# A fused delta-rule attention and MLP kernel: first keys loaded alone, weights and later chunks held back behind the first transposes, first chunk prepared in halves, PSUM banks of its own for the MLP

## The chip, the cores and the metric

The kernel runs on one core of one Trainium2 chip. The metric is the device time of one execution in microseconds (us). Each time in this text is the median of several executions; a profile is one execution of the same program and gives its span, the time from the first to the last recorded instruction, which is about 2 us shorter than the time. The engines are TensorE (PE in the profile, with its weight loads as PEld), VectorE (DVE), ScalarE (ACT), GpSimd (POOL) and SyncE (SP), whose only work here is to issue DMAs.

## The reference, cut to what matters

```python
# 4 x 8 heads, 768 steps, head size 48; x is 3072 x 384
k_n = k / (norm(k, axis=-1) + 1e-06)
for t in range(768):                       # per head
    y[t]  = q[t] @ state
    state = state + beta[t] * outer(k_n[t], v[t] - state.T @ k_n[t])
x = y as rows of tokens, 8 heads side by side        # 3072 x 384
h = x @ w_in                                         # 384 x 2048
out = gelu_tanh(h) @ w_out                           # 2048 x 384
```

The kernel computes the recurrence in 12 chunks of 64 steps. Within a chunk it inverts a small triangular matrix per head with 64x64 matmuls (two groups of heads, five rounds each). Every two chunks give 512 tokens, which the MLP can take as one tile, so there are 6 MLP tiles. The inputs are float32; the matmuls take bfloat16, and the 4-byte weights are cast on their way into SBUF.

## The kernel before

The program builds a list of operations, each with an estimated cost for each engine that may run it, what it reads and writes, and a priority. A list scheduler, at build time, then fixes **one order for each engine**. On the chip every engine goes through its order and waits, in order, on semaphores. So an instruction whose data is late holds up everything behind it on its engine. This holds for SP too: a DMA that must wait for its source, or for its buffer to be free, holds up all later DMAs of that queue.

```python
def load_step(c, pr):                       # keys, queries, values of chunk c; 3 buffers (RL = 3)
    s = c % RL
    for nm, t, src in (("kf", kf, k), ("qf", qf, q), ("vf", vf, v)):
        ...
        for a in range(2):                  # 2 DMAs of 192 KB each
            op({"sp": 0.6}, {"sp": f_dma(t[s][64 * a:64 * a + 64, :, :], sv[a, C * c:C * c + C, :, :])},
               writes=[f"{nm}{s}_{a}"], prio=pr, dma=f"d_{nm}{c}", lat=4.0)
...
load_step(0, -70)
... # beta
load_step(1, -60)
for kt in range(KT):                        # 3 DMAs issued by POOL, cast to bf16
    op({"pool": 1.2}, {"pool": f_dma(W1[:, kt, :], w1v[:, kt, :])}, writes=[f"W1{kt}"],
       prio=T(0, 15 + kt), dma="d_w1", lat=8.0)
for j in range(2):                          # 2 more
    op({"pool": 1.2}, {"pool": f_dma(W2[:, 8 * j:8 * j + 8, :], w2v[:, 8 * j:8 * j + 8, :])},
       writes=[f"W2{j}"], prio=T(0, 20 + j), dma="d_w2", lat=8.0)
...
def prep(c):        # square keys, reduce, root, reciprocal; KQ = normalised keys and queries in bf16
    ...
    op({"sp": 1.1}, {"sp": f_dma(KQT[i]..., KQ[i]..., True)},      # DMA transpose, 3 buffers (RB = 3)
       reads=[f"KQ{i}", f"KQq{i}"], writes=[f"KQT{i}"], prio=pr + 0.2, dma=f"d_T{c}", lat=4.0)
...
def mlp(t):
    pr = T(2 * t + 2, 0)                    # due when chunk 2t + 2 is
    ... # DMA transpose x -> xT, then 16 groups of 3 matmuls xT,W -> gelu -> gT, then gT,W2 -> out
...
prep(0)
prep(1)
for c in range(NCH):
    if c + 2 < NCH:
        load_step(c + 2, T(c - 1))          # nothing but its buffer and the order holds it back
        prep(c + 2)
    masks(c)
    for g in range(2):
        intra(c, g)                         # the 64x64 matmuls
    state(c)
    if c % 2 == 1:
        mlp(c // 2)
```

Below, T0, T1, T2 and T3 are the DMA transposes of the first four chunks' keys and queries (KQT<-KQ in the profile). No attention matmul of a chunk can start before its transpose has landed.

## Time and profile before

The time before was 345.34 us, the median of 3 runs (343.79 to 346.5).

The span cut in three, from the view of busy time by stretches. The cuts are the first attention matmul (the first that reads KQT) and the first MLP matmul (the first xT,W). A row gives the stretch in us, its length, then busy time and number of instructions of each engine, the granted TensorE clock as a share of full speed, the busy share of the 16 DMA engines, and GB/s. The DMA share is a sum of packet times and exceeds 1 in places here.

```profile
core 0: us, PE busy (x) PEld busy (x) DVE busy (x) ACT busy (x) POOL busy (x), PEclk, DMA share, GB/s
0.00:41.30 41.30, 1.69 (x10) 1.40 (x14) 6.87 (x21) 8.05 (x11) 13.71 (x19) 1.00 1.11 180
41.30:102.30 61.00, 38.47 (x1632) 34.85 (x1632) 41.68 (x65) 27.50 (x47) 34.49 (x23) 0.91 0.64 108
102.30:340.90 238.60, 226.67 (x5476) 137.16 (x5472) 132.48 (x201) 133.91 (x229) 72.22 (x49) 0.98 0.39 75
```

Three stages show. In the **head** (41.3 us) TensorE has only the small transposes of beta and the DMA engines are full. In the **ramp** (61.0 us) there is only attention work, and TensorE is busy 38.5 us of it. In the **rest** (238.6 us) MLP matmuls fill the gaps of the attention and TensorE is busy 226.7 us, 95%. Only there is it the bound.

What happens in the head, from the timeline of the kernel before (start, length in us, engine, line, instruction, output<-input; in brackets the idle time before it and what ended it; lines of SPq and POOL with DMA_ are DMAs being issued, not moved):

```profile
0.81 1.44 SPq L304 DMA_DIRECT2D kf<-in_k_dram  x2
1.78 1.86 POOL L304 DMA_DIRECT2D W<-in_moe_w_in_dram  x3
2.29 9.43 SPq L304 DMA_DIRECT2D qf<-in_q_dram  x2
3.61 1.82 POOL L304 DMA_DIRECT2D W<-in_moe_w_out_dram  x2
11.77 9.14 SPq L304 DMA_DIRECT2D vf<-in_v_dram  x2
15.20 0.84 ACT L289 ACTIVATE sq<-kf 128x768 f32<-128x768 f32 x1 [13.11 <-DMA kf<-in_k_dram]
36.22 3.45 SPq L303 DMA_TRANSPOSE KQT<-KQ  x1
41.26 1.07 PE L296 MATMUL ps<-KQT 48*64 48x128 bf16 x32 [12.20 <-DMA KQT<-KQ]
45.85 3.65 SPq L303 DMA_TRANSPOSE KQT<-KQ  x1
51.98 3.66 SPq L303 DMA_TRANSPOSE KQT<-KQ  x1
```

The first keys are issued at 0.81 us and can be used only at 15.20 us. The two issues of queries take 9.43 us of the SP queue, those of values 9.14 us. The weights are on their way at that time.

The end of the kernel, from the chain of waits (the work that ended last, followed back; start, length, what): the last MLP tile waits for its transpose with nothing else to do.

```profile
311.59 0.80 ACT x L289
312.41 0.81 ACT x L289
313.24 3.70 DMA xT<-x
316.99 20.95 PE ps L296 x112
```

### The profile page before, as it was taken

How to read it: one execution, taken by the hardware profiler on the slowest of the kernel's cores; microseconds unless marked ns; L12 is line 12 of the kernel's file. 1: busy time of each engine (PE TensorE's matmuls, PEld its weight loads, DVE VectorE, ACT ScalarE, POOL GpSimd, SP SyncE). 2: the span in 40 equal slices, each digit the busy share in tenths (PEclk: the TensorE clock that was granted, in tenths of full speed). 3: DMA queues.
4: the chain of work that ended last, by engine and by line, in shares of the span. 5: the costliest groups of instructions: out<-in, count | busy, mean ns of one | idle time of the engine just before them, and what ended most of it. 6: DMA issues, size and time to landing. Idle time of an engine off the chain costs nothing.

```text
span 340.9 us, 15121 instructions
## 1 busy us (share of the span) xinstructions
PE 266.8 (78%) x7110; PEld 173.4 (51%) x7110; DVE 181.0 (53%) x287; ACT 169.5 (50%) x286; POOL 120.4 (35%) x90
## 2 busy tenths in 40 slices
PE   0001125875769999898999699999999999999896
PEld 0001015764754556554567455566666655656353
DVE  2102255786774757676676554666757756642001
ACT  1202312665459753477534386554795447852640
POOL 5007266443679616057432660160252105000000
PEclk9999999999678999999999699999999999999999
DMA  7999999200899723937414923228042060002201
GB/s 132 193 195 190 189 193 185 44 6 11 139 165 178 133 49 94 177 73 115 91 50 65 193 45 64 50 64 184 10 53 38 26 96 4 4 4 69 71 23 70
DMA packets 116078, 31.83 MB, mean 93 GB/s; under 512 B 110512, under 2 KB 115632, under 8 KB 116016
## 3 DMA queue, kind: packets, MB, share of 16 engines
q1 hardware_dynamic: 113504, 27.73, 45.8%
q0 software_dynamic: 2512, 3.15, 5.3%
q8 instruction: 55, 0.90, 1.1%
q14 instruction: 7, 0.06, 0.1%
HBM read 20.64 MB, written 4.72 MB: 74 GB/s over the span
## 4 chain that ended last, share of the span: by engine, by line
PE 66%; SPq 12%; DMA 8%; ACT 5%; issue 3%; DVE 3%; POOL 1%
PE ps L296 64%; SPq L304 9%; DMA kf<-in_k_dram 7%; SPq L303 2%; ACT Z L289 2%; PE ps L571 2%; ACT x L289 1%; ACT sq L289 1%; DVE F L280 1%; DMA xT<-x 1%; POOL W L280 1%; DVE N L280 1%; DVE R L280 1%; POOL sq L280 0%; POOL Z L280 0%
## 5 line engine op out<-in xcount | busy, mean ns | idle before, releaser
L280 DVE TENSOR_TENSOR F<-twoI,ps 128x512 bf16<-128x512 bf16 x120 | 80.1, 683 | 55.1 <-PE ps L296 54.5
L296 PE MATMUL ps<-xT,W 128*128 128x512 bf16 x288 | 76.5, 391 | 1.7 <-DMA xT<-x 1.4
L289 ACT ACTIVATE Z<-ps 128x512 bf16<-128x512 f32 x96 | 55.3, 597 | 39.1 <-PE ps L296 38.7
L296 PE MATMUL ps<-W,gT 128*128 128x384 bf16 x384 | 69.2, 327 | 0.0
L289 ACT ACTIVATE gT<-ps 128x512 bf16<-128x512 f32 x96 | 56.8, 598 | 22.5 <-PE ps L296 21.0
L296 PE MATMUL ps<-X,Z 64*64 64x64 bf16 x1920 | 52.8, 201 | 8.9 <-ACT Z L289 4.8
L296 PE MATMUL ps<-Z,F 64*64 64x64 bf16 x1920 | 54.1, 201 | 7.2 <-issue 5.0
L280 POOL TENSOR_TENSOR W<-identB,N 128x512 bf16<-128x512 bf16 x21 | 24.2, 1151 | 95.3 <-DVE N L280 95.3
L296 PEld LDWEIGHTS ps<-Z,F 64*64 64x64 bf16 x1920 | 42.6, 115 | 28.7 <-DVE F L280 16.4
L296 PEld LDWEIGHTS ps<-X,Z 64*64 64x64 bf16 x1920 | 42.5, 116 | 25.0 <-ACT Z L289 13.9
L296 PEld LDWEIGHTS ps<-W,gT 128*128 128x128 bf16 x384 | 34.4, 98 | 22.0
L280 POOL TENSOR_TENSOR sr<-ss,half 128x16 f32<-128x16 f32 x9 | 26.4, 2932 | 29.1 <-DVE ss L478 29.1
L296 PEld LDWEIGHTS ps<-xT,W 128*128 128x128 bf16 x288 | 22.9, 99 | 24.5 <-issue 1.9
L285 DVE COPY osb<-ps 128x384 f32<-128x384 f32 x23 | 12.8, 557 | 39.0 <-PE ps L296 38.8
L289 ACT ACTIVATE sq<-kf 128x768 f32<-128x768 f32 x9 | 7.6, 842 | 42.9 <-DMA kf<-in_k_dram 42.9
L289 ACT ACTIVATE x<-ps 64x768 bf16<-64x768 f32 x24 | 19.3, 804 | 15.7 <-PE ps L296 15.3
L296 PE MATMUL ps<-KQT 48*64 48x128 bf16 x384 | 12.5, 246 | 18.5 <-DMA KQT<-KQ 17.5
L280 POOL TENSOR_TENSOR NU<-mU,bcol 128x1024 f32<-128x1024 f32 x12 | 23.7, 1976 | 1.0 <-DVE bcol L285 1.0
L289 ACT ACTIVATE TT<-ps 128x512 bf16<-128x512 f32 x24 | 14.1, 595 | 18.7 <-PE ps L296 18.6
L296 PE MATMUL ps<-identF,BL 128*128 128x128 f32 x6 | 1.6, 448 | 27.4 <-DMA BL<-in_beta_dram 27.4
L280 POOL TENSOR_TENSOR KQ<-kf,rn 128x768 bf16<-128x768 f32 x12 | 17.7, 1474 | 15.1 <-PE ps L296 9.8
L280 DVE TENSOR_TENSOR N<-ps,NU 128x512 bf16<-128x512 f32 x24 | 16.3, 686 | 11.8 <-PE ps L296 11.7
(48 smaller groups left out, 224.1 us busy)
## 6 DMA issues: line engine op xcount, KB each, us to landing
kf<-in_k_dram SPq DMA_DIRECT2D x24, 192.0 KB, 4.2
qf<-in_q_dram SPq DMA_DIRECT2D x24, 192.0 KB, 4.6
vf<-in_v_dram SPq DMA_DIRECT2D x24, 192.0 KB, 4.5
out_dram<-osb SPq DMA_DIRECT2D x24, 192.0 KB, 2.8
W<-in_moe_w_in_dram POOLq DMA_DIRECT2D x3, 512.0 KB, 8.6
W<-in_moe_w_out_dram POOLq DMA_DIRECT2D x2, 768.0 KB, 17.8
BL<-in_beta_dram SPq DMA_DIRECT2D x2, 96.0 KB, 4.5
KQT<-KQ SPq DMA_TRANSPOSE x12, 5.3
```

The source lines that it names most:

```text
L280: return lambda e: e.tensor_tensor(out() if callable(out) else out, a() if callable(a) else a, b() if callable(b) else b, op)
L285: return lambda e: e.tensor_copy(out, a() if callable(a) else a)
L289: return lambda e: e.activation(out, a() if callable(a) else a, func)
L296: ins = t.matmul(out, lhsT, rhs, start=st, stop=sp_, skip_group_check=skip)
L303: return lambda e: e.dma_start_transpose(out, a)
L304: return lambda e: e.dma_start(out, a)
L571: ins = t.transpose(bankb()[r, p, :], W[r, p, :], identB[r, :])
```

## The change

The intent was to start the attention early. The first keys are loaded alone, then beta, queries and the next keys. Weights wait: W1 for the second transpose (T1), W2 for the third (T2). The other loads of chunks 0 to 2 wait for the preparation of chunk 0 or 1. The first chunk is squared and multiplied in two halves on two engines. The MLP goes to the lowest priority and gets two PSUM banks of its own (6 for attention), all 8 for the last tile. The scheduler also gets a simple model of DMA bandwidth. The diff, cut to its core:

```diff
+BANKS = {"t": (0, 6), "f": (6, 8), "l": (0, 8)}
 ...
+            if o.dma:                                   # in the scheduler: transfers one after the other
+                dma_free = max(o.end + 1.3, dma_free) + o.bw
+                o.lat = dma_free + 0.5 - o.end
 ...
-        load_step(0, -70)
+        load("kf", 0, -70)
 ...     # beta
-        load_step(1, -60)
-        ... # W1 and W2 with no wait
+        load("qf", 0, -68)
+        load("kf", 1, -67)
 ...
+            parts = [slice(0, 8), slice(8, 16)] if c == 0 else [slice(0, NP)]
+            ... # square on ACT and POOL, product on DVE and POOL, one half each, for chunk 0
 ...
-            op(dict(d_pool2(512), dve=0.4), {"pool": ... W ...})        # and the same for Z
+            op({"dve": 0.42} if c < 2 else d_pool2(512), {"pool": ... W ...})
 ...
-            pr = T(2 * t + 2, 0)
+            pr = T(2 * t + 2, 1000)
+            mo = "f" if t < NT - 1 else "l"
 ...
         prep(0)
+        load("qf", 1, -40, ["KQ0", "KQx0", "KQq0"])                     # wait for chunk 0's keys and queries
+        load("vf", 0, -39, ["KQ0", "KQx0", "KQq0"])
         prep(1)
+        load("kf", 2, -38, ["KQ0", "KQx0", "KQq0"])
+        load("qf", 2, -37, ["KQ0", "KQx0", "KQq0"])
+        for kt in range(KT):
+            op({"pool": 0.9}, {"pool": f_dma(W1[:, kt, :], w1v[:, kt, :])}, reads=["KQT1"], writes=[f"W1{kt}"],
+               prio=-20 + kt, dma="d_w1", bw=2.8)
+        load("vf", 1, -15, ["KQ1", "KQq1"])
         for c in range(NCH):
             if c + 2 < NCH:
-                load_step(c + 2, T(c - 1))
+                for nm in ("kf", "qf", "vf"):
+                    if c > 0 or nm == "vf":
+                        load(nm, c + 2, T(c - 1), ["KQ1", "KQq1"] if c == 0 else [])
                 prep(c + 2)
+            if c == 0:
+                for j in range(2):
+                    op({"pool": 0.9}, {"pool": f_dma(W2[...], w2v[...])}, reads=["KQT2"], writes=[f"W2{j}"],
+                       prio=-5 + j, dma="d_w2", bw=4.2)
```

More of the change, by code (lines that the diff above doesn't have):

```diff
@@ L21 @@
     __slots__ = ("idx", "cost", "fns", "deps", "prio", "alloc", "uses", "dma", "lat",
-                 "eng", "start", "end", "count", "clock", "sync", "mode")
+                 "eng", "start", "end", "count", "clock", "sync", "mode", "bw")
 class Plan:
@@ L38, in __init__, with op @@
         self.users = {}
-    def op(self, cost, fns, reads=(), writes=(), prio=0.0, alloc=(), dma=None, lat=0.0, mode="t"):
+    def op(self, cost, fns, reads=(), writes=(), prio=0.0, alloc=(), dma=None, lat=0.0, mode="t", bw=0.0):
         o = Op()
         o.idx = len(self.ops)
-        o.cost, o.fns, o.prio, o.dma, o.lat, o.mode = cost, fns, prio, dma, lat, mode
+        o.cost, o.fns, o.prio, o.dma, o.lat, o.mode, o.bw = cost, fns, prio, dma, lat, mode, bw
         o.alloc = tuple(alloc)
@@ L89, in schedule @@
         pe_mode = "t"
+        dma_free = 0.0
         bank_free = [0.0] * self.nbanks
@@ L100, in dep_time, with find_banks @@
             return t
-        def find_banks(n, t0):
+        def find_banks(n, t0, lo, hi):
             best = None
-            for i in range(self.nbanks - n + 1):
+            for i in range(lo, hi - n + 1):
                 ts = bank_free[i:i + n]
@@ L135, in schedule @@
                                 bank_free[k] = None
-                            f = find_banks(n, t)
+                            f = find_banks(n, t, *BANKS[o.mode])
                             for k, x in sv:
@@ L148, in schedule @@
                     pr = o.prio
-                    if e == "pe" and o.mode != pe_mode:
+                    if e == "pe" and (o.mode == "t") != (pe_mode == "t"):
                         pr += KEEP
@@ L162, in schedule @@
             o = ops[i]
-            if e == "pe" and o.mode != pe_mode:
+            if e == "pe" and (o.mode == "t") != (pe_mode == "t"):
                 t += SWITCH
@@ L413, in bass_deltanet__then__act_gelu_tanh_kernel @@
             op({"dve": 0.7}, {"dve": lambda e, i=i: e.memset(KQ[i][:, :, :, D:64], 0.0)},
-               writes=[f"KQ{i}"], prio=-90 + i)
+               writes=[f"KQz{i}"], prio=-90 + i)
         const("identF", identF, 0.0, ALU.not_equal, 1.0, [[-1, 128]], 1)
@@ L425, in bass_deltanet__then__act_gelu_tanh_kernel, with load @@
            reads=IDI, writes=["twoI"], prio=-80)
-        def load_step(c, pr):
+        def load(nm, c, pr, after=()):
+            t, src = {"kf": (kf, k), "qf": (qf, q), "vf": (vf, v)}[nm]
             s = c % RL
-            for nm, t, src in (("kf", kf, k), ("qf", qf, q), ("vf", vf, v)):
-                sv = src.rearrange("b h s d -> (b h) s d").rearrange("(p a) s d -> a s p d", a=2)
-                for a in range(2):
-                    op({"sp": 0.6}, {"sp": f_dma(t[s][64 * a:64 * a + 64, :, :], sv[a, C * c:C * c + C, :, :])},
-                       writes=[f"{nm}{s}_{a}"], prio=pr, dma=f"d_{nm}{c}", lat=4.0)
+            sv = src.rearrange("b h s d -> (b h) s d").rearrange("(p a) s d -> a s p d", a=2)
+            for a in range(2):
+                op({"sp": 0.65}, {"sp": f_dma(t[s][64 * a:64 * a + 64, :, :], sv[a, C * c:C * c + C, :, :])},
+                   reads=after, writes=[f"{nm}{s}_{a}"], prio=pr, dma=f"d_{nm}{c}", bw=1.05)
         STEP = 28.0
@@ L440, in bass_deltanet__then__act_gelu_tanh_kernel @@
         bfl = beta.rearrange("b h (c r) -> (b h c) r", r=C).rearrange("(t n) r -> n t r", n=128)
-        load_step(0, -70)
+        load("kf", 0, -70)
         for dup in range(2):
-            op({"sp": 0.6}, {"sp": f_dma(BL[:, :, dup, :], bfl)}, writes=[f"BL{dup}"], prio=-69, dma="d_BL", lat=3.0)
-        load_step(1, -60)
-        w1v = moe_w_in.rearrange("(kt p) f -> p kt f", p=128)
-        w2v = moe_w_out.rearrange("(fc p) e -> p fc e", p=128)
-        for kt in range(KT):
-            op({"pool": 1.2}, {"pool": f_dma(W1[:, kt, :], w1v[:, kt, :])}, writes=[f"W1{kt}"],
-               prio=T(0, 15 + kt), dma="d_w1", lat=8.0)
-        for j in range(2):
-            op({"pool": 1.2}, {"pool": f_dma(W2[:, 8 * j:8 * j + 8, :], w2v[:, 8 * j:8 * j + 8, :])},
-               writes=[f"W2{j}"], prio=T(0, 20 + j), dma="d_w2", lat=8.0)
+            op({"sp": 0.65}, {"sp": f_dma(BL[:, :, dup, :], bfl)}, writes=[f"BL{dup}"], prio=-69, dma="d_BL", bw=0.4)
+        load("qf", 0, -68)
+        load("kf", 1, -67)
         W1N = [f"W1{kt}" for kt in range(KT)]
@@ L474, in prep @@
             kn = [f"kf{s}_0", f"kf{s}_1"]
-            op({"pool": 1.5, "act": 0.82}, {"pool": f_tt(sq[j][:, :, :], kf[s][:, :, :], kf[s][:, :, :], ALU.mult),
-                                            "act": f_act(sq[j][:, :, :], kf[s][:, :, :], ACT.Square)},
-               reads=kn, writes=[f"sq{j}"], prio=pr)
-            op({"dve": 0.95}, {"dve": lambda e: e.tensor_reduce(ss[j][:, :], sq[j][:, :, :], AX.X, ALU.add)},
-               reads=[f"sq{j}"], writes=[f"ss{j}"], prio=pr)
+            parts = [slice(0, 8), slice(8, 16)] if c == 0 else [slice(0, NP)]
@@ new lines, in prep @@
+            for n, u in enumerate(parts):
+                w = 1.0 / len(parts)
+                cost = {"pool": 1.5 * w, "act": 0.82 * w + 0.05}
+                cost = {"act": cost["act"]} if c < 2 and n == 0 else {"pool": cost["pool"]} if c < 2 else cost
+                op(cost, {"pool": f_tt(sq[j][:, u, :], kf[s][:, u, :], kf[s][:, u, :], ALU.mult),
+                          "act": f_act(sq[j][:, u, :], kf[s][:, u, :], ACT.Square)},
+                   reads=kn, writes=[f"sq{j}{n}"], prio=pr)
+                op({"dve": 0.95 * w}, {"dve": lambda e, u=u: e.tensor_reduce(ss[j][:, u], sq[j][:, u, :], AX.X, ALU.add)},
+                   reads=[f"sq{j}{n}"], writes=[f"ss{j}{n}"], prio=pr)
@@ L480, in prep @@
+            ssn = [f"ss{j}{n}" for n in range(len(parts))]
             if c < NSQ:
                 op({"act": 0.24}, {"act": f_act(sr[j][:, :], ss[j][:, :], ACT.Sqrt)},
-                   reads=[f"ss{j}"], writes=[f"sr{j}"], prio=pr)
+                   reads=ssn, writes=[f"sr{j}"], prio=pr)
             else:
                 op({"pool": 2.95}, {"pool": f_tt(sr[j][:, :], ss[j][:, :], half[:, :], ALU.pow)},
-                   reads=[f"ss{j}", "half"], writes=[f"sr{j}"], prio=pr)
+                   reads=ssn + ["half"], writes=[f"sr{j}"], prio=pr)
@@ L486, in prep @@
             op({"dve": 0.1}, {"dve": lambda e: e.tensor_scalar(ss[j][:, :], sr[j][:, :], 1e-6, None, op0=ALU.add)},
-               reads=[f"sr{j}"], writes=[f"ss{j}"], prio=pr)
+               reads=[f"sr{j}"], writes=ssn, prio=pr)
             op({"dve": 0.25}, {"dve": lambda e: e.reciprocal(rn[j][:, :], ss[j][:, :])},
-               reads=[f"ss{j}"], writes=[f"rn{j}"], prio=pr)
-            op(d_pool2(NP * D), {"pool": f_tt(KQ[i][:, 0, :, 0:D], kf[s][:, :, :],
-                                              rn[j][:, :].unsqueeze(2).to_broadcast([128, NP, D]), ALU.mult)},
-               reads=kn + [f"rn{j}"], writes=[f"KQ{i}"], prio=pr)
+               reads=ssn, writes=[f"rn{j}"], prio=pr)
@@ L493, in prep @@
+            for n, u in enumerate(parts):
+                w = 1.0 / len(parts)
+                f = f_tt(KQ[i][:, 0, u, 0:D], kf[s][:, u, :],
+                         rn[j][:, u].unsqueeze(2).to_broadcast([128, NP // len(parts), D]), ALU.mult)
+                op({"dve": 0.9 * w} if c == 0 and n == 0 else {"pool": 1.5 * w}, {"pool": f, "dve": f},
+                   reads=kn + [f"rn{j}", f"KQz{i}"], writes=[f"KQ{i}" if n == 0 else f"KQx{i}"], prio=pr)
             op({"pool": 0.85, "act": 0.82}, {"pool": f_cp(KQ[i][:, 1, :, 0:D], qf[s][:, :, :]),
@@ L494, in prep @@
                                              "act": f_act(KQ[i][:, 1, :, 0:D], qf[s][:, :, :])},
-               reads=[f"qf{s}_0", f"qf{s}_1", f"KQ{i}"], writes=[f"KQq{i}"], prio=pr + 0.1)
+               reads=[f"qf{s}_0", f"qf{s}_1", f"KQz{i}"], writes=[f"KQq{i}"], prio=pr + 0.1)
             op({"sp": 1.1}, {"sp": f_dma(KQT[i].rearrange("p k m t -> p (k m) t"),
                                          KQ[i].rearrange("p k n d -> p (k n d)"), True)},
-               reads=[f"KQ{i}", f"KQq{i}"], writes=[f"KQT{i}"], prio=pr + 0.2, dma=f"d_T{c}", lat=4.0)
+               reads=[f"KQ{i}", f"KQq{i}"] + ([f"KQx{i}"] if c == 0 else []), writes=[f"KQT{i}"], prio=pr + 0.2 if c > 1 else -50 + c, dma=f"d_T{c}", bw=1.5)
@@ L543, in intra @@
                                        mU[:, :].unsqueeze(1).unsqueeze(1).to_broadcast([128, 4, 2, C]), ALU.mult)},
-               reads=[h] + MASKU, writes=[f"DT{i}{g}"], prio=pr + 0.2)
-            op(dict(d_pool2(512), dve=0.4), {"pool": f_tt(W[:, :, :], bc(identB), N[:, :, :], ALU.add),
+               reads=[h] + MASKU, writes=[f"DT{i}{g}"], prio=pr + 0.35)
+            op({"dve": 0.42} if c < 2 else d_pool2(512), {"pool": f_tt(W[:, :, :], bc(identB), N[:, :, :], ALU.add),
                                             "dve": f_tt(W[:, :, :], bc(identB), N[:, :, :], ALU.add)},
                reads=[nm["N"], "identB"], writes=[nm["W"]], prio=pr + 0.3)
-            op(dict(d_pool2(512), dve=0.4), {"pool": f_tt(Z[0][:, :, :], bc(identB), N[:, :, :], ALU.subtract),
+            op({"dve": 0.42} if c < 2 else d_pool2(512), {"pool": f_tt(Z[0][:, :, :], bc(identB), N[:, :, :], ALU.subtract),
                                             "dve": f_tt(Z[0][:, :, :], bc(identB), N[:, :, :], ALU.subtract)},
@@ L653, in ku @@
                     return r
-                op(mm_pe(32, D, 4), {"pe": f_mms(ku)}, reads=[f"KQ{i}", f"U{j2}"], writes=[h3], alloc=[(h3, 2)], prio=pr)
+                op(mm_pe(32, D, 4), {"pe": f_mms(ku)}, reads=[f"KQ{i}", f"U{j2}"] + ([f"KQx{i}"] if c == 0 else []), writes=[h3], alloc=[(h3, 2)], prio=pr)
                 def sv(t):
@@ L689, in mlp @@
         def mlp(t):
-            pr = T(2 * t + 2, 0)
+            pr = T(2 * t + 2, 1000)
             op({"sp": 1.1}, {"sp": f_dma(xT[:, t % 2, :, :], x[:, t % 2, :, :].rearrange("q b e -> q (b e)"), True)},
                reads=[f"x{t % 2}_{h}{a}" for h in range(2) for a in range(2)], writes=[f"xT{t % 2}"], prio=pr - 10,
-               dma=f"d_x{t}", lat=4.0)
+               dma=f"d_x{t}", bw=1.5)
+            mo = "f" if t < NT - 1 else "l"
             xv = xT[:, t % 2, :, :].rearrange("q (b kt) n -> q kt b n", kt=KT)
@@ L701, in m1 @@
                             for kt in range(KT)]
-                op({"pe": 0.65}, {"pe": f_mms(m1)}, mode="f", reads=[f"xT{t % 2}"] + W1N, writes=[h], alloc=[(h, 1)],
+                op({"pe": 0.65}, {"pe": f_mms(m1)}, mode=mo, reads=[f"xT{t % 2}"] + W1N, writes=[h], alloc=[(h, 1)],
                    prio=pr + fc * 2.4)
@@ L711, in m2 @@
                                  fc == FC - 1, False) for fc in range(8 * part, 8 * part + 8)]
-                    op({"pe": 1.3}, {"pe": f_mms(m2)}, mode="f",
+                    op({"pe": 1.3}, {"pe": f_mms(m2)}, mode=mo,
                        reads=[f"gT{t % 2}_{fc}" for fc in range(8 * part, 8 * part + 8)] + W2N + ([h] if part else []),
@@ L721, in mlp @@
                 op({"sp": 0.6}, {"sp": f_dma(out[row0:row0 + 128, :], osb[o_][:, :])}, reads=[f"osb{o_}"],
-                   prio=pr + 42 + b * 4, dma=f"d_o{t}_{b}", lat=3.0)
+                   prio=pr + 42 + b * 4, dma=f"d_o{t}_{b}", bw=1.0)
         prep(0)
+        load("qf", 1, -40, ["KQ0", "KQx0", "KQq0"])
+        load("vf", 0, -39, ["KQ0", "KQx0", "KQq0"])
         prep(1)
+        load("kf", 2, -38, ["KQ0", "KQx0", "KQq0"])
+        load("qf", 2, -37, ["KQ0", "KQx0", "KQq0"])
+        w1v = moe_w_in.rearrange("(kt p) f -> p kt f", p=128)
+        w2v = moe_w_out.rearrange("(fc p) e -> p fc e", p=128)
+        for kt in range(KT):
+            op({"pool": 0.9}, {"pool": f_dma(W1[:, kt, :], w1v[:, kt, :])}, reads=["KQT1"], writes=[f"W1{kt}"],
+               prio=-20 + kt, dma="d_w1", bw=2.8)
+        load("vf", 1, -15, ["KQ1", "KQq1"])
         for c in range(NCH):
             if c + 2 < NCH:
-                load_step(c + 2, T(c - 1))
+                for nm in ("kf", "qf", "vf"):
+                    if c > 0 or nm == "vf":
+                        load(nm, c + 2, T(c - 1), ["KQ1", "KQq1"] if c == 0 else [])
                 prep(c + 2)
+            if c == 0:
+                for j in range(2):
+                    op({"pool": 0.9}, {"pool": f_dma(W2[:, 8 * j:8 * j + 8, :], w2v[:, 8 * j:8 * j + 8, :])},
+                       reads=["KQT2"], writes=[f"W2{j}"], prio=-5 + j, dma="d_w2", bw=4.2)
             masks(c)
```

## The prediction

> **What bounds it now.** The page gives PE 267 us busy of a 340.9 us span. By stretches (busy time by window) TensorE is the bound only after 102 us: 102.3 to 313 us PE 203 of 211 us; 317 to 338 us (the last MLP tile alone) 20.9 of 21. Before that it starves: one small beta transpose until 41.3 us, then 8.6 of 20.8 us (41.3 to 62) and 30.0 of 40.3 us (62 to 102.3). Of about 74 us of idle PE, 60 lie before 102 us and some 8 in the last 28.
>
> The chain of waits up to 67 us is the SP DMA queue and key loads. In the DMA view a key load lands in about 4 us, but the first took 13.6: the weights, 3+2 issues on POOL at 1.8 to 5.4 us, are moved at the same time. The SP queue's issues then take 9.4, 9.1 us (timeline), so the first values land at 26.7 and beta at 27.4 us, and POOL, held in order by the value copy, forms the first normalised keys only at 27.5 us. More loads go ahead of the first transpose: issued 36.2, landed 41.3. The Trainium skill, "DMA: Bandwidth & Descriptors", section "Queues, rings and completion order", says each DMA engine round-robins between queue rows by packet; the 13.6 against 4 us agrees.
>
> **What the change does.** Same matmuls, same bytes; order only.
> 1. First keys alone: landing near 5.5 us. Then half square 0.5, half reduce 0.5, table load 1.3, root 0.2, small ops 0.5, half product 0.75 (halves of 0.84, 0.95, 1.47): normalised at 9 to 9.5 us, queries about then, transpose 5 us: first KQT matmul at 14 to 16 us, not 41.3. Estimate: 26 us, all on the critical path.
> 2. Later transposes before at +10 and +16.5 us after the first, should come at +6 and +12; weights (about 6.3 MB, 33 us at the 190 GB/s seen) move beneath the first chunks and are needed 40 us later. The attention-only ramp from first transpose to first MLP matmul (61 us, delayed by in-order engines blocked on key loads and transposes) shrinks to about 50, half offset by more idle or slow-paced PE.
> 3. MLP at lowest priority: attention runs ahead, the end is MLP tiles only. The 3.7 us wait for xT and the serial x copies (1.6 us) before the last tile vanish: 4 us.
> 4. Cost: two MLP banks, so first-layer groups cycle at (0.65 PE + 0.25 + 0.6 ACT)/2, about 0.78 us instead of 0.65, where no attention fills; 2 us per such tile, estimate 4 to 6 us. Six banks for attention, W and Z on POOL (1.15 against 0.42 us): hidden.
> PE work after the first MLP matmul is about 226 us in both.
>
> **Sum.** First KQT 15, ramp 52, PE work 226, residual idle 12, drain 3: span near 308; with the 1.7 to 4.4 us between span and time, **311 us**, range 298 to 325. Faster by over 2%: 0.95; within: 0.03; slower: 0.02.
>
> **What would show it.** First KQT matmul at 14 to 16 us (timeline); first xT,W matmul at 60 to 72 us; PE over 95% from there; no xT wait in the chain; attention's last matmul well before the end, more than one MLP tile after it; ACT gT activations spaced 0.78 us there. Total PE busy about 260 to 270.
>
> **What would make it wrong.** The fixed order waiting on loads that land later than planned, POOL blocked by weight issues that wait for a transpose; attention-first order making PE wait for short-latency results while MLP work is ready; bank starvation; more throttling of the clock than the dips seen (0.78, 0.83); or, upward, a much shorter ramp (MLP at 50 us: below 300).

## More of the kernel before

The view of the DMA queues for 4.3 to 13.2 us, the stretch of the W1 packets, shows who had the 16 engines (queue q0 carries the weights issued by POOL, q1 everything that SP issues; packets, MB, share of the 16 engines in the stretch):

```profile
q0 software_dynamic: 514, 1.63, 94.6%
q1 hardware_dynamic: 682, 0.13, 10.9%
```

## The result

The kernel after took **331.97 us** (median of 4 runs, 330.95 to 332.88) against 345.17 us (4 runs, 343.79 to 346.5) of the kernel before on the same chip. The ratio is **0.9617** with a 95% interval of 0.9568 to 0.9665. Ratios in this text are the mean time of one kernel's runs over that of the other's of the same rounds, so not quite the ratio of the quoted medians. Executions over 1.5% slower than the fastest of the same kernel are left out of the means. The kernel is faster by 3.8%, but the range that was predicted (298 to 325 us) does not hold it: 21 us of the predicted gain of 34 us are missing.

The same three stages, after:

```profile
0.00:15.10 15.10, 1.65 (x6) 1.35 (x6) 6.37 (x20) 5.21 (x7) 8.32 (x13) 1.00 0.79 140
15.10:98.20 83.10, 53.08 (x1809) 46.97 (x1810) 53.68 (x80) 34.77 (x57) 42.04 (x30) 0.86 1.09 174
98.20:328.80 230.60, 221.87 (x5299) 133.61 (x5296) 121.27 (x181) 133.40 (x226) 75.83 (x54) 0.99 0.34 66
```

The head shrank by 26 us, as foreseen. The ramp grew by 22 us, to 83.1 us, and that is where the gain went. The rest is 8 us shorter. Of these 8 us some 5 are not a gain: 176 more attention matmuls had been done in the ramp (1808, as the 1809 shown take in one MLP matmul at the edge, less 1632), and TensorE's busy time in the rest is 4.8 us less (226.67 - 221.87). Of the ramp's growth of 22.1 us, 14.6 are busy time of TensorE (53.08 - 38.47), far more than 176 matmuls need, and 7.5 are waiting; "The clock" comes back to this. The DMA share of the ramp rose from 0.64 to 1.09: the DMA engines, which were full in the head before, are now full in the ramp.

The timeline after, the lines that answer to those shown of before and the places where the ramp stands still:

```profile
10.20 3.09 SPq L308 DMA_TRANSPOSE KQT<-KQ  x1
15.12 1.07 PE L301 MATMUL ps<-KQT 48*64 48x128 bf16 x32 [7.02 <-DMA KQT<-KQ]
22.80 4.36 SPq L308 DMA_TRANSPOSE KQT<-KQ  x1
31.36 1.85 POOL L309 DMA_DIRECT2D W<-in_moe_w_in_dram  x3
31.56 0.67 SPq L309 DMA_DIRECT2D qf<-in_q_dram  x1
32.28 8.41 SPq L309 DMA_DIRECT2D vf<-in_v_dram  x2
44.19 0.84 ACT L294 ACTIVATE KQ<-qf 128x768 bf16<-128x768 f32 x1 [9.56 <-DMA qf<-in_q_dram]
45.57 0.63 PE L301 MATMUL ps<-X,Z 64*64 64x64 bf16 x16 [7.46 <-ACT X L294]
46.70 3.75 SPq L308 DMA_TRANSPOSE KQT<-KQ  x1
56.39 11.62 SPq L308 DMA_TRANSPOSE KQT<-KQ  x1
98.19 1.46 PE L301 MATMUL ps<-xT,W 128*128 128x512 bf16 x3
```

T0 is issued at 10.20 us instead of 36.22, and the first attention matmul starts at 15.12 us instead of 41.26. T1 follows 12.6 us later, T2 36.5 us later. Before, the distances were 9.6 and 15.8 us (36.22, 45.85 and 51.98 us). The picture of the old head comes back at 31 us: the weights are issued, the next SP issues take 8.41 us, and one load of queries lands 12.6 us after its issue. ScalarE waits 9.56 us for these queries, and TensorE waits 7.46 us behind ScalarE. T3 takes 11.62 us of the SP queue while W2 is moved.

The chain of waits of the kernel after goes through the same load, and its end is TensorE without a wait, from 295.85 us on the MLP alone:

```profile
31.56 12.60 DMA qf<-in_q_dram
...
292.07 33.83 PE ps L301 x259
```

And the view of the DMA queues for the W1 packets after, 33.4 to 42.7 us:

```profile
q0 software_dynamic: 430, 1.57, 88.3%
q1 hardware_dynamic: 1562, 0.30, 19.0%
```

In both kernels W1 takes about nine tenths of the engines for some 9 us, and the SP queue gets 0.13 MB in 8.9 us before and 0.30 MB in 9.3 us after: 15 and 32 GB/s. When the SP queue is alone, as from 22 to 31 us after, it moves 1.48 MB in 9 us, 164 GB/s:

```profile
q1 hardware_dynamic: 7130, 1.48, 117.7%
```

The lead of the kernel after tells the same: 26.1 us at the first attention matmul, but 4.1 us at the first MLP matmul (102.31 against 98.19). With the 5 us of attention work done ahead that is some 9 us.

### The profile page after: what moved, and what is told of

Its sections match the earlier page's. It is cut to its first block, busy times and chain, and to the rows that moved or that the text cites. A ratio compares the mean times of both kernels' runs of the same rounds, so it can differ in the third digit from the quotient of the medians.

```text
span 328.8 us, 15129 instructions
## 1 busy us (share of the span) xinstructions
PE 276.6 (84%) x7110; PEld 181.9 (55%) x7110; DVE 181.3 (55%) x281; ACT 173.4 (53%) x289; POOL 126.2 (38%) x96
## 3 DMA queue, kind: packets, MB, share of 16 engines
q0 software_dynamic: 2512, 3.15, 5.7%
## 4 chain that ended last, share of the span: by engine, by line
PE 62%; DMA 11%; DVE 10%; SPq 5%; POOL 4%; issue 4%; ACT 3%
PE ps L301 60%; SPq L309 4%; DMA kf<-in_k_dram 4%; DMA qf<-in_q_dram 4%; DMA KQT<-KQ 3%; DVE F L285 3%; DVE N L285 2%; PE ps L578 2%; POOL W L285 1%; ACT Z L294 1%; DVE ss L490 1%; SPq L308 1%; DVE Z L285 1%; POOL sr L285 1%; DVE ss L481 1%
## 5 line engine op out<-in xcount | busy, mean ns | idle before, releaser
L285 DVE TENSOR_TENSOR F<-twoI,ps 128x512 bf16<-128x512 bf16 x120 | 81.2, 684 | 60.0 <-PE ps L301 59.1
L294 ACT ACTIVATE gT<-ps 128x512 bf16<-128x512 f32 x96 | 56.9, 597 | 27.5 <-PE ps L301 26.1
L301 PE MATMUL ps<-X,Z 64*64 64x64 bf16 x1920 | 57.3, 206 | 15.0 <-ACT X L294 8.2
L301 PEld LDWEIGHTS ps<-X,Z 64*64 64x64 bf16 x1920 | 45.9, 121 | 33.4 <-ACT X L294 12.6
L301 PE MATMUL ps<-Z,F 64*64 64x64 bf16 x1920 | 56.5, 206 | 5.4 <-DVE F L285 5.1
L301 PEld LDWEIGHTS ps<-Z,F 64*64 64x64 bf16 x1920 | 45.2, 120 | 25.6 <-DVE F L285 18.7
L285 POOL TENSOR_TENSOR KQ<-kf,rn 128x768 bf16<-128x768 f32 (+1 forms) x12 | 17.1, 1422 | 71.0 <-PE ps L301 67.0
L285 POOL TENSOR_TENSOR W<-identB,N 128x512 bf16<-128x512 bf16 x20 | 23.1, 1155 | 35.7 <-DVE N L285 35.1
L301 PEld LDWEIGHTS ps<-xT,W 128*128 128x128 bf16 x288 | 22.1, 98 | 19.9 <-issue 0.5
L285 POOL TENSOR_TENSOR NU<-mU,bcol 128x1024 f32<-128x1024 f32 x12 | 23.6, 1970 | 2.1 <-DVE N L285 2.1
L285 POOL TENSOR_TENSOR Z<-identB,N 128x512 bf16<-128x512 bf16 x20 | 23.1, 1156 | 0.0
L294 ACT ACTIVATE X<-ps 128x512 bf16<-128x512 bf16 x24 | 14.1, 594 | 14.9 <-PE ps L578 14.8
L285 DVE TENSOR_TENSOR DT<-ps,mU 128x512 bf16<-128x512 f32 x24 | 18.4, 768 | 0.4
```

The lines of the kernel that those rows point to most:

```text
L285: return lambda e: e.tensor_tensor(out() if callable(out) else out, a() if callable(a) else a, b() if callable(b) else b, op)
L294: return lambda e: e.activation(out, a() if callable(a) else a, func)
L301: ins = t.matmul(out, lhsT, rhs, start=st, stop=sp_, skip_group_check=skip)
```

## The experiments

Twelve kernels were run, in three batches on three chips; each batch has its own runs of the kernel before, with medians of 346.55, 344.41 and 349.01 us. To put them side by side this text gives **scaled times**, the ratio times 345.17 us; the intervals of the ratios are mostly 0.5% to 1% either way, so a scaled time is good to 2 to 3.5 us. The letters and numbers in the quoted expectations are the working names and estimates of the moment; the sentence ahead of each says in plain words what was to be told apart.

The reasons that were on the table for the missing 21 us:

- **Weights.** They had cost their time in the head and now cost it in the ramp, as the ramp is bound by DMA too.
- **Order of one instruction.** ScalarE's cast of the late queries (chunk 3), or T2's place behind loads in the SP queue, blocks engines that could go on.
- **Later loads.** Chunks 3 to 8 are loaded as soon as buffers come free, long before they are needed, and crowd out what is needed.
- **Banks.** The MLP's two banks or its low priority cost something.
- **Clock.** The granted clock of the ramp fell from 0.91 to 0.86, and a matmul takes longer there.

### Weights taken almost away, in both kernels

These two give a wrong result: only the first 128 columns of W1 and the first two blocks of 128 rows of W2 are loaded, and they are used throughout. All instructions stay in their places; only the bytes shrink, to a sixteenth for W1 and an eighth for W2. If the weights' cost had been removed by the change, the kernel after would gain nothing from it. If it had only moved, both would gain about the same. (Where the expectation speaks of 6.3 MB, it means the float32 bytes that are read; the records of the DMA engines count the 3.15 MB that are written as bfloat16.)

```diff
-f_dma(W1[:, kt, :], w1v[:, kt, :])
+f_dma(W1[:, kt, 0:128], w1v[:, kt, 0:128])
-f_dma(W2[:, 8 * j:8 * j + 8, :], w2v[:, 8 * j:8 * j + 8, :])
+f_dma(W2[:, j, :], w2v[:, j, :])
# matmuls read W1[:, kt, 0:128] and W2[:, fc // 8, :]
```

> The changed kernel, its order on every engine untouched, but the five weight loads move a tenth of their bytes (0.6 of 6.3 MB; every MLP matmul then reads the same slice, so the result is wrong on purpose and PE work is unchanged). Theory A (the bytes of the weights, moved while the fixed order has key, query and value loads for later chunks and the second, third and fourth transposes in one SP queue, delay those transposes and hold ACT in its place for a query load): the 9.6 us wait of ACT for queries at 34.6 to 44.2 us falls under 2 us, the third transpose is issued before 38 us instead of 46.7, the first MLP matmul comes near 80 us instead of 98.2, and the time falls by 12 to 20 us. Rival C (the order itself: attention before MLP, two banks, in-order engines waiting on each other): time falls by less than 4 us and the first MLP matmul stays after 93 us. Rival D (the slower matmul pace in the ramp): no change either.

> The kernel before with the same cut of the weights' bytes, order untouched, wrong result on purpose. If the weights sharing the engines with the first key load were the cause of the late start, the first key lands near 5 us instead of 15, the first KQT matmul comes near 24 us instead of 41.3 (the remaining loads ahead of it in the queue still cost about 1 us each), and the time falls by about 15 us. If instead it was the order of the SP queue alone, the first KQT matmul stays after 35 us and the time falls by less than 6 us.

Measured: the kernel after with tiny weights 320.03 us, ratio to before 0.9234 (0.9166 to 0.9303); the kernel before with tiny weights 330.89 us, ratio 0.9577 (0.9512 to 0.9641). The falls in time came as expected. Not all else did (by a profile of a slow execution): the first MLP matmul after came at 89.1 us, not near 80, ScalarE's wait for the queries shrank to 3.09 us, not under 2, and T2 was issued at 40.72 us, not before 38. Scaled:

| | full weights | tiny weights | cost of the weights |
|---|---|---|---|
| before | 345.2 | 330.6 | 14.6 |
| after | 332.0 | 318.7 | 13.3 |
| gain of the change | 13.2 | 11.9 | |

This is the central result. **The weights cost 14.6 us before and 13.3 us after**, the same within the 2 to 3 us of the intervals. The change did not hide them; it moved them. The stretches of the two show where the cost sat. First the kernel before with tiny weights, then the kernel after with tiny weights (this profile fell in an execution that counts as slow, 323.38 us, so its stretches are only a sketch):

```profile
0.00:26.40 26.40, 1.65 (x6) 1.36 (x6) 6.88 (x21) 8.05 (x11) 12.95 (x19) 1.00 1.05 173
26.40:90.90 64.50, 38.50 (x1633) 34.61 (x1633) 41.41 (x65) 28.01 (x47) 34.98 (x24) 0.88 0.63 105
```

```profile
0.00:15.60 15.60, 1.65 (x6) 1.36 (x6) 6.49 (x20) 5.21 (x7) 8.29 (x13) 1.00 0.83 135
15.60:89.10 73.50, 54.77 (x1808) 48.91 (x1808) 51.47 (x80) 34.84 (x57) 40.95 (x31) 1.00 0.94 158
```

Before, the tiny weights shorten the head by 14.9 us (41.3 to 26.4) and not the ramp (61.0 to 64.5). After, they shorten the ramp by 9.6 us (83.1 to 73.5) and not the head. So of the 26.1 us by which the change brings the first attention matmul forward, 14.9 us come from getting the weights out of the way, and most of this is paid back in the ramp; 11.3 us (26.4 to 15.1) come from the order of loads and the halves.

Tiny weights leave the ramp of the kernel after at 73.5 us, with a DMA share of 0.94. There is more than the weights.

### The change in two parts

Loads and preparation alone: the kernel after with all 8 banks for everything and the old MLP priority. MLP part alone: the kernel before with the banks and the low priority.

```diff
# e3, against after
-BANKS = {"t": (0, 6), "f": (6, 8), "l": (0, 8)}
+BANKS = {"t": (0, 8), "f": (0, 8), "l": (0, 8)}
-            pr = T(2 * t + 2, 1000)
+            pr = T(2 * t + 2, 0)
# e4, against before: the reverse, with find_banks(n, t, lo, hi) and the mode "l" for the last tile
```

> The changed kernel with the MLP part undone: all eight banks for both, MLP priority as before; loads, prep halves and DMA model stay. Theory A: the loss sits in the loads, so the first MLP matmul stays late (90 to 100 us) and the time is within 4 us of the changed kernel (328 to 338). Rival C (attention-first order and two banks are what costs): the first MLP matmul comes before 80 us and the time falls by 10 us or more, to about 320.

> The kernel before with only the MLP part of the change: banks split 6 and 2 (all 8 in the last tile) and MLP at lowest priority. Theory A: the MLP part is worth a few us by itself (no xT wait before the last tile, which was 3.7 us plus the serial copies), so 338 to 345. Rival C: it is slower than before, 348 to 360.

Measured: loads alone 336.17 us, ratio 0.9715 (0.9659 to 0.977), scaled 335.3. That is 9.9 of the 13.2 us, and its ramp is 78.1 us, so the long ramp is not the banks' doing. The MLP part adds some 3.4 us to it. The MLP part alone took 355.14 us, ratio 1.0225 (1.0129 to 1.032): slower, within the 348 to 360 us of the rival in its expectation and not the 338 to 345 us of the favoured reading, a miss (that it is slower by 2% is not sure, as the interval begins at 1.3%). The same edit is worth +3 us in one kernel and -8 us in another. The cause of the loss was not followed up, but one thing is plain in its chain of waits: in the order that the scheduler made of this edit alone, the x copies (0.80 and 0.81 us) and the wait for xT (3.65 us) still stand bare before the last tile, so the gain at the end did not come.

### The order of one instruction

Three edits of the finished order of the kernel after, each a pure move: ScalarE's cast of chunk 3's queries behind its first x copies; T2 right behind T1 in the SP queue; both.

```diff
         P.schedule()
+        move("act", "KQq0", 1, "x0_01", 0)     # e5, e7: 2nd writer of KQq0 behind the 1st of x0_01
+        move("sp", "KQT2", 0, "KQT1", 0)       # e6, e7: T2 behind T1
```

> The changed kernel with one instruction moved: ACT's cast of the queries of chunk 3 goes from before chunk 1's X copy to behind chunk 0's two x copies; every other engine's order untouched. Theory A1 (ACT, in order, stands 9.6 us before a query load that shares the engines with the first weights, and PE stands 7.5 us behind it): ACT's wait and PE's 7.5 us gap at 38 to 45.6 us vanish, but the third transpose, issued at 46.7 us, then holds PE, so the first MLP matmul comes 2 to 6 us earlier and the time falls 2 to 6 us. Theory A2 (the SP queue alone: transposes behind the bulk loads): no change, within 2 us.

> The changed kernel with one instruction moved in the SP queue: the third transpose goes from behind ten loads of later chunks to right behind the second transpose; nothing else. It is issued near 28.5 us instead of 46.7. Theory A1: no gain, as ACT still stands before the query load of chunk 3 (even 1 to 3 us later): time within 3 us of the changed kernel. Theory A2: gain of 5 us or more.

> Both moves together. Theory A (a chain of two head-of-line blocks, each hiding the other): more than the sum of the two alone, first MLP matmul 7 to 12 us earlier, time 322 to 327. Rival C or D: as the changed kernel, within 3 us.

Measured: 330.92 us (ratio 0.9569, 0.9503 to 0.9634), 335.18 us (0.9686, 0.9609 to 0.9763) and 334.68 us (0.9666, 0.9586 to 0.9747), against 0.9617 of the kernel after. None differs from it beyond the intervals; the expected 322 to 327 us of both moves together is missed. The timelines tell why. One line each of the first, the second and the third, the longest wait of ScalarE in the ramp:

```profile
49.74 0.84 ACT L294 ACTIVATE sq<-kf 128x768 f32<-128x768 f32 x1 [9.00 <-DMA kf<-in_k_dram]
```

```profile
47.69 0.84 ACT L294 ACTIVATE KQ<-qf 128x768 bf16<-128x768 f32 x1 [12.99 <-DMA qf<-in_q_dram]
```

```profile
52.31 0.84 ACT L294 ACTIVATE sq<-kf 128x768 f32<-128x768 f32 x1 [12.20 <-DMA kf<-in_k_dram]
```

Take away the instruction that waits for a late load, and the next one waits for the next late load: 9.56 us in the kernel after, 9.00, 12.99 and 12.20 us here. The theory of one badly placed instruction falls. What is short is the supply, not the order of these two.

### Later loads held back

A gate for each load from chunk 3 on: it waits until the transpose of the chunk before it has landed.

```diff
-                        load(nm, c + 2, T(c - 1), ["KQ1", "KQq1"] if c == 0 else [])
+                        load(nm, c + 2, T(c - 1), ["KQ1", "KQq1"] if c == 0 else [f"KQT{(c + 1) % RB}"])
```

> The cause taken away in the scheduler: loads of chunk c from 3 on wait until the transpose of chunk c-1 has landed, so the SP queue never holds loads of chunks 3 to 8 ahead of the second to fourth transposes (in the changed kernel about 17 MB have moved by 98 us). Theory A: third transpose issued before 32 us, first MLP matmul at 62 to 75 us, time 305 to 318. If the ramp is bound by the bytes that the first chunks and the weights need, or by the pace of the in-order engines (rivals B, C), the first MLP matmul stays after 85 us and the time above 322.

> The gated kernel (g1_gated, 325.5 us, first MLP matmul 78.0 us) with the weight loads cut to a tenth of their bytes, order untouched, wrong result on purpose. Theory W (while weight packets are queued, the SP queue gets next to nothing: in the changed kernel 0.4 us of engine time in 35 to 40 us against 4.8 for the weights; so the weights shut the ramp out for their own 19 us wherever they fall in it): the third transpose lands 5 us after its issue instead of 14.6, PE's mid-group gaps in the ramp (9.9 us, put down to issue) shrink under 4, first MLP matmul before 66 us, time 308 to 316. Rival B (key, query and value bytes and in-order waits alone bound the ramp once it is gated): first MLP matmul after 72 us, time within 4 us of 325.5.

The second of these is the same with tiny weights, again with a wrong result. Measured: gated 325.49 us (5 runs), ratio 0.9423 (0.9351 to 0.9495), scaled 325.3; gated with tiny weights 317.4 us, ratio 0.9151 (0.9048 to 0.9254), scaled 315.9. Both miss a part of what was expected: the gate alone has its first MLP matmul at 78.0 us and not at 62 to 75, and 325 us and not 305 to 318; with tiny weights the first MLP matmul is at 70.4 us and not before 66, while the time comes near the expected 308 to 316. The stretches of the head, ramp and rest with the gate, and of the ramp alone with the gate and tiny weights:

```profile
0.00:14.20 14.20, 1.65 (x6) 1.36 (x6) 6.40 (x20) 5.20 (x7) 7.38 (x13) 1.00 0.80 143
14.20:78.00 63.80, 42.49 (x1440) 37.57 (x1440) 40.41 (x61) 25.84 (x43) 23.97 (x19) 0.76 0.95 140
78.00:320.70 242.70, 227.29 (x5664) 139.31 (x5664) 134.10 (x201) 142.64 (x242) 94.45 (x63) 0.98 0.44 86
```

```profile
14.10:70.40 56.30, 39.91 (x1441) 34.77 (x1441) 40.66 (x62) 26.13 (x44) 23.21 (x19) 0.78 0.65 108
```

Between 15 and 95 us the SP queue moves 10.55 MB in the kernel after and 6.60 MB with the gate (view of the DMA queues). The first MLP matmul comes at 78.0 us instead of 98.2, though with 368 fewer attention matmuls done by then, and the gain in time is 6.7 us. Held back and with tiny weights, the ramp is 56.3 us and the gain on the kernel after is 16.1 us, less than 13.3 and 6.7 added up. The gate lets the scheduler build a new order for every engine, so its 6.7 us cannot be put down to the held bytes alone. The two runs of this section have one order; between them the weights cost 9.4 us (325.3 - 315.9).

These two runs also show the weights' effect on one instruction, in the same order and at the same moment. First the gated kernel: T2 is issued at 27.28 us, and the load behind it, which waits for T2 to land, at 41.84 us. Then the same with tiny weights: 27.46 and 33.77 us.

```profile
27.20 1.86 POOL L309 DMA_DIRECT2D W<-in_moe_w_in_dram  x3
27.28 3.84 SPq L308 DMA_TRANSPOSE KQT<-KQ  x1
41.84 1.32 SPq L309 DMA_DIRECT2D kf<-in_k_dram  x2
```

```profile
27.38 1.83 POOL L309 DMA_DIRECT2D W<-in_moe_w_in_dram  x3
27.46 3.29 SPq L308 DMA_TRANSPOSE KQT<-KQ  x1
33.77 1.32 SPq L309 DMA_DIRECT2D kf<-in_k_dram  x2
```

One transpose and its queue are held for 14.6 us beside the full weights and for 6.3 us beside the tiny ones.

### Weights in quarters

If the weights' bytes cannot be avoided, they can be spread: W1 in four column quarters, W2 in four row quarters, each with its own semaphore, released by T2's landing (half of W1), by the first x copies (the other half) and by the first xT (W2). A first-layer matmul waits only for its own quarter, a second-layer one for its own two. Once on top of the gated loads, once without them, and once with the gate but with the MLP's banks and priority put back.

```diff
+WGATES = {"KQT2": [W1 quarters 0, 1], "x0_01": [W1 quarters 2, 3], "xT0": [W2 quarters 0 to 3]}
+f_dma(W1[:, :, 512 * n:512 * n + 512], w1v[:, :, 512 * n:512 * n + 512])    reads=[gate], writes=[f"W1{n}"]
+f_dma(W2[:, 4 * n:4 * n + 4, :], w2v[:, 4 * n:4 * n + 4, :])                reads=[gate], writes=[f"W2{n}"]
-  reads=[xT] + W1N                  # first layer
+  reads=[xT, f"W1{fc // 4}"]
-  reads=[gT ...] + W2N              # second layer
+  reads=[gT ..., f"W2{2 * part}", f"W2{2 * part + 1}"]
```

> The gated kernel with the weights in quarters behind later gates: two quarters of the first weights behind the third transpose's landing, two behind chunk 0's x copies, the second weights behind the landing of the first x transpose; MLP groups wait only for their own quarter. Theory W: shut-outs are short and fall where no transpose is in flight, first MLP matmul at 62 to 70 us, time 310 to 320. If the weights cost the same wherever they are: within 3 us of 325.5.

> The changed kernel with the quarters and gates for the weights, but the loads of later chunks not gated. Theory W with premature loads as a second cause of its own: between, 322 to 329. If the premature loads alone are the cause: within 3 us of 332. If the weights alone: as g2_quarters.

> g2_quarters with the MLP part undone (eight shared banks, MLP priority as before). In the changed kernel that part was worth 4 us (336 without it), in the kernel before it cost 9 us. If attention-first with split banks pays wherever the loads are early: 3 to 8 us slower than g2_quarters. If its worth is an accident of the order: within 3 us or faster.

Measured: gate and quarters **322.09 us**, ratio **0.9269** (0.9206 to 0.9331), scaled 319.9, with a correct result. It beats both kernels, and the gated one by 5.4 us; the first MLP matmul, at 75.9 us, missed the expected 62 to 70. The quarters also cut W1's packets (1536 of 1024 bytes in place of 384 of 4096, by the trace's records), so the later gates and the smaller packets are not told apart. Quarters without the gate took 335.18 us, ratio 0.9646 (0.9583 to 0.9708), scaled 333.0: nothing gained on the kernel after, against an expected 322 to 329 us, a miss. Its ramp had a DMA share of 1.00; with the premature loads still there, weights that come later seem to meet a queue that is just as full (argued from this share, not shown by a run of its own). Gate and quarters without the MLP part took 325.05 us, ratio 0.9359 (0.9276 to 0.9442), scaled 323.0, so the MLP part is worth 3 us here too, a difference no larger than the intervals.

The stretches of the best kernel, ramp and rest:

```profile
14.30:75.90 61.60, 44.97 (x1521) 39.53 (x1522) 40.98 (x64) 29.17 (x48) 27.63 (x21) 0.75 0.86 136
75.90:321.00 245.10, 226.03 (x5586) 138.20 (x5584) 130.27 (x195) 139.72 (x239) 92.87 (x65) 0.99 0.45 88
```

### All runs side by side

| kernel | time, us | ratio to before | scaled, us | first attention matmul | first MLP matmul |
|---|---|---|---|---|---|
| before | 345.2 | 1 | 345.2 | 41.3 | 102.3 |
| after | 332.0 | 0.9617 | 332.0 | 15.1 | 98.2 |
| e1, after, tiny weights (wrong) | 320.0 | 0.9234 | 318.7 | 15.6 | 89.1 |
| e2, before, tiny weights (wrong) | 330.9 | 0.9577 | 330.6 | 26.4 | 90.9 |
| e3, loads only | 336.2 | 0.9715 | 335.3 | 15.3 | 93.4 |
| e4, MLP part only | 355.1 | 1.0225 | 352.9 | 41.5 | 97.3 |
| e5, cast later | 330.9 | 0.9569 | 330.3 | 15.3 | 98.9 |
| e6, T2 first | 335.2 | 0.9686 | 334.3 | 15.6 | 100.6 |
| e7, both moves | 334.7 | 0.9666 | 333.6 | 14.9 | 100.2 |
| g1, gated loads | 325.5 | 0.9423 | 325.3 | 14.2 | 78.0 |
| e8, gated, tiny weights (wrong) | 317.4 | 0.9151 | 315.9 | 14.1 | 70.4 |
| g2, gate and quarters | 322.1 | 0.9269 | 319.9 | 14.3 | 75.9 |
| e9, quarters only | 335.2 | 0.9646 | 333.0 | 15.5 | 90.5 |
| e10, g2 without the MLP part | 325.1 | 0.9359 | 323.0 | 14.4 | 80.3 |

### The clock

No run was made for it; the runs at hand answer for the recorded clock, but not for the pace of the matmuls. The four runs of the kernel after had mean granted clocks of 0.958, 0.902, 0.984 and 0.897 and times of 330.95, 332.88, 331.57 and 332.36 us: 9% of clock, 0.6% of time. The ramp ran at a recorded clock of 1.00 in the quarters without gate (335 us) and at 0.75 in the best kernel (322 us). So the recorded clock does not set the time. The Trainium skill, "TensorE: Matmul & The Clock Gate", Part 1, says that the throttled state is the default and activity releases the throttle. The records agree only in part: the rest, where TensorE is 96% busy, shows 0.99 and the ramp 0.86, but the head before, where it is busy 1.7 of 41.3 us, shows 1.00.

Nor is the recorded clock the pace. The group of 16 matmuls shown above at 45.57 us of the kernel after took 0.63 us, at a recorded clock of 1.00 (45 to 50 us). In the rest such a group mostly takes 0.42 to 0.44 us:

```profile
149.95 0.42 PE L301 MATMUL ps<-Z,F 64*64 64x64 bf16 x16
```

**This slower pace is a rival that no run took away.** A matmul of the ramp has 29.3 ns of busy time after (53.08 us by 1809) and 23.6 ns before (38.47 us by 1632); by these figures some 10 us (an estimate) of the ramp's growth are pace. It is not how the weights or the later loads cost their time: with tiny weights a matmul took 30.3 ns (54.77 us by 1808) and with the gate 29.5 (42.49 by 1440), and both kernels were faster. How much of the rest of the missing gain it holds stays open.

## Why the prediction was wrong, point by point

**Point 1, the head: right.** The prediction put the first attention matmul at 14 to 16 us; it came at 15.12. The reasons hold too: keys alone, halves, then the transpose. What the prediction missed is where the 26 us came from. It knew that the weights delayed the first keys; it did not ask which part of the 26 us was the weights' (14.9 us by the run with tiny weights) and would have to be paid elsewhere.

**Point 2, the ramp: this is the step that failed.** In its words: "weights ... move beneath the first chunks and are needed 40 us later. The attention-only ramp ... shrinks to about 50". It measured 83.1 us, of which about 5 us are attention work done ahead. Transposes were to come at +6 and +12 us after the first and came at +12.6 and +36.5; the first MLP matmul was to come at 60 to 72 us and came at 98.2. Two things took the place of the step:

- The weights did not move beneath anything. The ramp itself lives on the SP queue: loads, transposes, x. The weights took nearly all of the 16 engines for about 9 us (W1, 88 to 95%) and most of them for 12 us (W2, 84% after), at 33.4 to 42.7 and 57.1 to 69.5 us after, and cost 13.3 us of time by the pair of runs with tiny weights, against 14.6 us before. That they are needed later helps only if nothing else needs the DMA meanwhile.
- The loads of later chunks, freed early by the faster start, filled what was left. Holding them back, with the new order that this brings, gained 6.7 us; both causes together gave 16.1 of the missing 21 us (332.0 - 311).

The prediction named a neighbour of this under what would make it wrong ("the fixed order waiting on loads that land later than planned"), with no size.

**Point 3, the end: right.** Attention's last group of matmuls starts at 295.2 us, 33.6 us before the end (before: 310.9 us, 30.0 us before it), there is no wait for xT, and more than one tile of MLP follows. The MLP part was put at 4 us; 3.4 us by the run without it, with intervals as wide as that.

**Point 4, the two banks: not seen.** The 4 to 6 us for slower first-layer groups did not show. While attention runs, it fills the gaps, and the last tile has all banks: its 48 xT,W matmuls took 10.5 us in both kernels. The rest is 96% busy (221.87 of 230.6 us), as the prediction said (over 95%).

**The sum.** Predicted: 15 + 52 + 226 + 12 + 3 = 308 us of span. Measured: 15.1 + 83.1 + 221.9 + 8.7 (idle and end of the rest together) = 328.8. The ramp was off by +31 us, the TensorE work behind it by -4, idle and end by -6. The total of busy TensorE, 276.6 us, was over the predicted 260 to 270; the slower pace of the ramp is in it.

**What stays open.** The gated kernel with tiny weights is at 315.9 us scaled, with an interval of 312.3 to 319.4; the predicted 311 lies just below it, some 5 us away. Its ramp is 56.3 us rather than 52. Two candidates were not tested. One is the pace of the matmuls, 27.7 ns in this ramp (39.91 us by 1441) against 23.6 before. The other is TensorE's waits called "issue", waits for which the profile shows no releaser: 4.3 us in this ramp, 9.9 us in the gated one with full weights, a difference of 5.6 of the 9.4 us that the weights cost there. Over the span the kernel after has 8.0 us of them, in pieces of up to 3.15 us, and the kernel before 10.5 us, so they do not set these two apart. They fall in the middle of groups of matmuls, where there is nothing to wait for. By the trace's records each of them in the two kernels (12 before, 11 after) ends 1.2 to 1.7 us after a transfer of DMA queue q8 ("instruction", 55 transfers of some 16 KB) has ended. That suggests that TensorE waits for instructions, but no run took this away, so it is not shown. A full DMA is not needed for it: before, waits of 0.94, 1.56 and 1.56 us between 73 and 82 us fall where the DMA share is 0.00.

## What to carry to other kernels

When a start is held up by a transfer, do not count its time as gained by postponing it: here 14.6 us of cost became 13.3. Before counting on it, look at the DMA share of the stage it moves into, and measure the transfer's cost by shrinking its bytes in both kernels with the order unchanged. Loads that are held back by nothing but a free buffer followed the faster start forward here and filled the DMA (10.55 MB against 6.60 MB on the SP queue from 15 to 95 us); gate them by need. When moving the one waiting instruction only makes the next one wait, stop tuning the order and look at the supply.

## What the Trainium skill lacked or had wrong

- "DMA: Bandwidth & Descriptors", section "Queues, rings and completion order", says that each DMA engine goes round the queue rows it has work for, a packet at a time. The traces show both queues moving at once, but not whose turn it is. The page does not say how unequal the shares become when packets differ in size, a term that the prediction lacked. Here W1's packets of 4096 bytes took 335 to 341 ns each in the two kernels' records and those of the SP queue beside them 18 to 23 ns. In the W1 stretch after, q1 moved 1562 packets beside 430 of q0, 3.6 to one, and had 19.0% of the engines' time against 88.3%. The stream with the large packets left the other queue 15 to 32 GB/s, against 164 alone.
- The same page, section "Issuing engines are not separate DMA queues", says that all issuers share the same 16 engines and that issuing from several saves only the sequencer's time, "which is usually small relative to the DMA itself". The sharing agrees. The issue time does not stay small under load: two issues took 1.44 us on an idle DMA and 9.43 or 8.41 us beside the weights, and one transpose 11.62 us instead of 3.09. As the SP queue goes in order, that time is lost for every transfer behind it.
- The same page, section "SWDGE vs HWDGE vs iDMA", says that a cast in a DMA must be issued by GpSimd. This kernel does it so, on a queue of its own (q0). What the page lacks is the price of such a load beside an urgent one of SP: with W1 issued at 1.78 us beside the first keys, ScalarE could square these only at 15.20 us; in the same order with tiny weights it did so at 6.15 us, and with the keys alone at 5.66 us.
- How long an engine waits for its instructions has no figure in "Runtime: NRT & Kernel Launch", section "Instruction fetch mechanics", where it would belong. The waits of TensorE called "issue", 10.5 us before and 8.0 us after in pieces of up to 3.15 us, each ended 1.2 to 1.7 us after a transfer of the queue named "instruction"; no run here settled the cause.
